# Three PSUM tiles cut by hand become one tile per buffer, and each weight block gets a DRAM tensor of its own

## The chip, the core and the metric

The kernel runs on one core of a Trainium2 chip. The metric is the device time of one execution in microseconds; the time before is the median of three runs.

## What is computed

An attention with a packed middle step feeds two matrix-multiply layers. Everything is float32 outside; inside, each operand of a large product is split into a rounded upper part and a small lower part, and three products (upper-upper, upper-lower, lower-upper) are added up in PSUM.

```python
# attention: 8 batches x 8 heads, 576 rows of 64, 32 packing rows
p_packed = sm_attn(p, k, v)               # softmax attention
out      = sm_attn(q, p_packed, p_packed)
x = out.transpose(0, 2, 1, 3).reshape(4608, 512)
# layer 1: 512 -> 2048 -> 512
h = x @ w_in
g = (a[0] + a[1]*h + a[2]*h**2 + a[3]*h**3) / (1 + abs(b[0])*abs(h) + abs(b[1])*h**2 + 1e-6)
x = g @ w_out
# layer 2: 512 -> 2048 -> 512
h = x @ w2_in
g = h * cos(h)
return g @ w2_out
```

## The kernel before, in words

The program is a list of steps (`add`), each with its engine, the objects that it reads, writes and makes, and the slots that its objects may take. `Plan.order` goes through an order of the steps per engine that is written out as numbers (`ORDER`), gives each new object a free slot (`make`), and emits the instructions in the order of the planned starts. Each engine runs its own list in order. The waits between engines are not written by hand: the framework derives them from the tiles that an instruction reads and writes.

PSUM has eight banks of 2 KB per partition. Before the change they are held by these tiles: `b2` (8192 bytes, four banks), `acc01` and `acc23` (two banks each, the latter in the place of the attention's `one0` and `one1`, which are tiles of their own, made anew for each use). `PART` says which slot is which slice of which tile, and `make` cuts the slice out by hand.

- Attention (the first 130 us, and parts of it later): `trans` (L946) transposes on TensorE into a slot of `tr`, that is `b2_0` or `b2_1`, the two halves of `b2`; `copied` (L950, ScalarE) reads it. `scores` (L973) writes the same slots; `max1`, `exp1`, `turn2` (L985, L991, L1050) read them. The transposes of exponents (L1008) and of small tiles (L960) write `one0` and `one1`.
- Layer 1 (128 items, up to about 1088 us): `front` (L1215) multiplies an attention half with folded weights into `b2_0` or `b2_1`, in turn; `absolute` (L1387) and `lin` (L1377) on ScalarE and `cubic` (L1382, L1384) on VectorE read the result. The rest of the rational function works in SBUF. `back` (L1235) adds the item into one of four accumulators `acc0` to `acc3`; at the end of a group `done1` (L1252 on ScalarE, L1250 on VectorE) empties them. `m_prod` (L1182) folds weights into a half of `b2`, emptied by L1191 and L1195.
- Layer 2 (six chunks of 768 tokens, eight quads each, from about 1088 us): in a quad, `part2` (L1270) makes seven products of six matmuls with 384 columns (a seven-product form of a two by two block product). Products 1, 6, 7 and 4 go one after another into one buffer A (slot `hA`, the first bank of `b2`), and after each of them `from_A` (L1280, ScalarE) copies A out; products 2, 5 and 3 go into a buffer B (slot `hB`, the second bank of `b2`), which `plus_B` (L1285, VectorE) adds to the copy. Then four cells of h times cos h run in SBUF (L1288 to L1316), and `back2` (L1324) adds each cell into three of six accumulators `six0` to `six5`. `six0` to `six3` lie in `acc01` and `acc23`, `six4` and `six5` in the third and fourth bank of `b2`. At the end of a chunk `done2` (L1335, L1337) empties all six.

The split weight blocks of layer 2 are written to DRAM during layer 1 (`b_keep`, L867) and read back for every quad (`b_back`, L870), seven blocks of 256 KB, into ten slots (`rg`) ahead of use. Before the change the seven blocks of a quad are slices of one DRAM tensor `w2[i]`, 128 rows of 14 KB, of which a block takes 2 KB.

Steps on engine "-" (`opening`) make slots available once the steps named have been issued, such as those of layer 2 in the place of layer 1's.

Of the kernel before, what the change touches and what calls it, by code (L numbers as in the profile page):

```python
# [10 lines left out]
F32 = mybir.dt.float32  # L11
# [565 lines left out]
def pack_attention_moe_moe_kernel(  # L577
# [14 lines left out]
    nc = tc.nc  # L592
# [1163 lines left out]
```

## Time and profile before

| what | us |
|---|---|
| median of three runs | 1967.95 |
| lowest, highest | 1960.86, 1969.67 |
| the profiled execution | 1970.45 |
| its span, from the first to the last instruction | 1968.7 |
| mean granted TensorE clock, share of full speed | 0.946 |

The profiled execution is the one that all rows come from; 1.75 us of its time lie outside the span. PE is TensorE's matmuls, PEld its weight loads, DVE VectorE, ACT ScalarE, POOL GpSimd, SP the engine that issues the DMAs. A group is written as line, engine, operation, output tile <- input tiles. Tiles appear by the program's names without numbers: `b` is the tile `b2`, `acc` is `acc01` or `acc23`, `one` is `one0` or `one1`, `ep` is the SBUF tile of the layers' work, `wo` and `g` the operands of `back` and `back2`. An idle time is put down to the instruction whose end released the engine. Matmul ends are modelled: a matmul's duration (0.3 to 0.4 us here) is longer than the distance to the next one, and after a wait the idle time shown is shorter than what the stream of matmuls lost.

### The profile page before, as it was taken

How to read it: one execution, taken by the hardware profiler on the slowest of the kernel's cores; microseconds unless marked ns; L12 is line 12 of the kernel's file. 1: busy time of each engine (PE TensorE's matmuls, PEld its weight loads, DVE VectorE, ACT ScalarE, POOL GpSimd, SP SyncE). 2: the span in 40 equal slices, each digit the busy share in tenths (PEclk: the TensorE clock that was granted, in tenths of full speed). 3: DMA queues.
4: the chain of work that ended last, by engine and by line, in shares of the span. 5: the costliest groups of instructions: out<-in, count | busy, mean ns of one | idle time of the engine just before them, and what ended most of it. 6: DMA issues, size and time to landing. Idle time of an engine off the chain costs nothing.

```text
span 1968.7 us, 28677 instructions
## 1 busy us (share of the span) xinstructions
PE 1665.3 (85%) x10416; PEld 1404.5 (71%) x10416; DVE 1376.1 (70%) x2434; ACT 1266.0 (64%) x2331; POOL 313.7 (16%) x287
## 2 busy tenths in 40 slices
PE   6666788887888888888898999988988888898988
PEld 3444577776877877777787777777777777776776
DVE  3445677878878878777887897667657657666665
ACT  4455667867777877777786776556556556556554
POOL 1222332212332322222220001001001000000000
PEclk8566899989999999999999999999999999999999
DMA  7545322323233112121125545335334434433431
GB/s 239 180 161 163 116 80 74 99 87 110 85 109 118 61 48 85 59 82 55 56 81 178 191 145 156 101 97 156 102 99 130 126 102 121 131 99 101 124 99 49
DMA packets 145165, 219.14 MB, mean 111 GB/s; under 512 B 25216, under 2 KB 77952, under 8 KB 145024
## 3 DMA queue, kind: packets, MB, share of 16 engines
q1 hardware_dynamic: 144448, 216.53, 36.3%
q8 instruction: 82, 1.34, 0.3%
q10 hardware_dynamic: 576, 0.79, 0.1%
q14 instruction: 59, 0.48, 0.1%
HBM read 173.21 MB, written 44.04 MB: 110 GB/s over the span
## 4 chain that ended last, share of the span: by engine, by line
PE 61%; ACT 18%; DVE 16%; issue 4%; DMA 1%; SPq 0%; DVEq 0%; ACTq 0%
PE b L1270 18%; PE acc L1324 12%; PE b L1215 11%; PE b L1324 7%; PE acc L1235 5%; DVE ep L1384 4%; ACT ep L1377 3%; DVE ep L1382 3%; ACT ep L1387 3%; PE b L946 3%; ACT ep L1280 3%; DVE ep L1285 2%; PE b L1182 2%; ACT ep L1390 2%; PE b L973 2%
## 5 line engine op out<-in xcount | busy, mean ns | idle before, releaser
L1235 PE MATMUL acc<-g,wo 128*128 128x288 f32 x3072 | 449.2, 300 | 23.2 <-ACT ob L1252 11.6
L1235 PEld LDWEIGHTS acc<-g,wo 128*128 128x128 f32 x3072 | 423.9, 191 | 52.4 <-ACT ob L1252 17.7
L1324 PE MATMUL acc<-wo,g 128*128 128x512 f32 x1152 | 306.3, 395 | 1.2 <-ACT st L1337 1.0
L1324 PEld LDWEIGHTS acc<-wo,g 128*128 128x128 f32 x1152 | 214.1, 188 | 32.8 <-ACT st L1337 1.4
L1280 ACT COPY ep<-b 128x384 f32<-128x384 f32 x192 | 91.9, 479 | 207.1 <-PE b L1324 117.0
L1296 DVE SCALAR_TENSOR_TENSOR ep<-ep 128x384 f32<-128x384 f32 x384 | 214.0, 559 | 6.7
L1396 POOL TENSOR_TENSOR ep<-ep 128x576 f32<-128x576 f32 x108 | 153.5, 1427 | 359.1 <-ACT ep L1390 130.0
L1324 PE MATMUL b<-wo,g 128*128 128x512 f32 x576 | 169.6, 408 | 42.4 <-ACT ep L1280 40.4
L1285 DVE TENSOR_TENSOR ep<-ep,b 128x384 f32<-128x384 f32 x144 | 79.6, 553 | 139.5 <-PE b L1324 89.9
L1324 PEld LDWEIGHTS b<-wo,g 128*128 128x128 f32 x576 | 101.1, 188 | 86.4 <-ACT ep L1280 72.6
L1288 ACT ACTIVATE ep<-ep 128x384 f32<-128x384 f32 x192 | 100.4, 524 | 85.8 <-DVE ep L1285 83.7
L1382 DVE TENSOR_TENSOR ep<-ep,b 128x576 f32<-128x576 f32 x128 | 93.9, 751 | 79.9 <-ACT ep L1387 40.4
L1310 DVE TENSOR_TENSOR ep<-ep 128x384 f32<-128x384 f32 x192 | 106.5, 557 | 58.1 <-ACT ep L1306 57.7
L1387 ACT ACTIVATE ep<-b 128x576 f32<-128x576 f32 x128 | 82.7, 648 | 96.9 <-PE b L1215 72.1
L1316 DVE TENSOR_TENSOR g<-ep,g 128x384 fp32r<-128x384 f32 x192 | 107.8, 563 | 42.1 <-ACT g L1313 41.9
L1215 PE MATMUL b<-a,sl2a 128*128 128x288 f32 x480 | 102.8, 326 | 38.5 <-DVE ep L1384 22.4
L1377 ACT ACTIVATE ep<-b,par 128x576 f32<-128x576 f32 x128 | 103.5, 828 | 44.6 <-PE b L1215 25.8
L1270 PE MATMUL b<-sr,a 128*128 128x384 f32 x518 | 115.9, 348 | 19.1 <-DVE ep L1285 11.0
L1384 DVE SCALAR_TENSOR_TENSOR ep<-ep,par,b 128x576 f32<-128x576 f32 x128 | 100.9, 810 | 43.9 <-PE b L1215 18.6
L1313 ACT CAST g<-ep 128x384 fp32r<-128x384 f32 x192 | 98.3, 513 | 48.8 <-DVE ep L1310 48.8
L1270 PE MATMUL b<-sr,sl2a 128*128 128x384 f32 x486 | 109.5, 350 | 19.3 <-DVE ep L1285 12.1
L1215 PE MATMUL b<-a,sr 128*128 128x288 f32 x576 | 95.6, 323 | 29.5 <-DVE ep L1384 12.2
(170 smaller groups left out, 3079.4 us busy)
## 6 DMA issues: line engine op xcount, KB each, us to landing
a<-w SPq DMA_DIRECT2D x135, 256.0 KB, 2.7
sl2a<-w SPq DMA_DIRECT2D x133, 256.0 KB, 2.7
sr<-w SPq DMA_DIRECT2D x68, 256.0 KB, 2.7
st<-in_moe_w_out_dram SPq DMA_DIRECT2D x32, 512.0 KB, 4.1
st<-in_moe_w_in_dram SPq DMA_DIRECT2D x30, 512.0 KB, 4.5
w<-fx SPq DMA_DIRECT2D x56, 256.0 KB, 2.0
x<-ob SPq DMA_DIRECT2D x24, 576.0 KB, 3.4
k_in<-in_k_dram SPq DMA_DIRECT2D x16, 576.0 KB, 5.4
```

What stands on the lines that cost most here:

```text
L1215: nc.tensor.matmul(TILE["h", j][:, e, 0:HS], lhsT=w[:, o : o + P], rhs=x[:, g, :], start=n == 0, stop=n == 3 * NG - 1,)
L1235: nc.tensor.matmul(o, lhsT=w, rhs=x, start=i == first and n == 0, stop=i == last and n == len(todo) - 1,)
L1270: nc.tensor.matmul(o, lhsT=u[:, ks], rhs=x[:, k, :], start=n in FRESH and k == 0 and j == 0, stop=k == KC // 2 - 1 and j == 2, skip_group_ ...
L1280: nc.scalar.copy(TILE["H", c, i, f, t], TILE["A", c, i][:, 0:W2])
L1285: nc.vector.tensor_tensor(H, H, B, op=ALU.add)
L1296: return nc.vector.scalar_tensor_tensor(Y, T, (-C1, -C2)[e], (TILE["H", *q], Y)[e], op0=ALU.mult, op1=ALU.add)
L1324: nc.tensor.matmul(o, lhsT=u[:, ms], rhs=x, start=FIRST2[c, t] == (i, f) and n == 0, stop=LAST2[c, t] == (i, f) and n == 2,)
L1377: nc.scalar.activation(shaped(j, "T"), hidden(j), AF.Identity, scale=par[:, 3:4], bias=par[:, 2:3])
L1382: nc.vector.tensor_tensor(T, T, h, op=ALU.mult)
L1384: nc.vector.scalar_tensor_tensor(T, T, par[:, 1:2], h, op0=ALU.add, op1=ALU.mult)
L1387: nc.scalar.activation(shaped(j, "V"), hidden(j), AF.Abs)
L1396: return side("denom", j).tensor_tensor(Q, Q, V, op=ALU.mult)
```

## The change

Each PSUM buffer becomes a tile of its own. Where a slot has no slab, `make` now asks the pool for a new tile under the slot's tag. `b2_0` and `b2_1` become tiles of two banks in the pool `ps2`, `acc0` to `acc3` tiles of one bank. For layer 2 the pool `ps2` is closed and a pool `ps4` opened in its place (`open_z`), with the tiles `hA`, `hB`, `six4` and `six5`; `six0` to `six3` use the tags of `acc0` to `acc3`. `open_z` runs once all steps `absolute`, `lin` and `cubic` have been issued, and `hA`, `hB`, `six4`, `six5` are free from then on; before, `hA` and `hB` came with the last `front`, and all of `six` with the first accumulator group that ended.

In DRAM `w2[i]` becomes seven tensors of 128 rows of 2 KB, one for each block.

The new opening step shifts the numbers of all later steps by one. Read with that shift, the order differs from before only in the passage from layer 1 to layer 2: 115 of 1760 TensorE steps change places, by at most 18 places, 188 of ScalarE's, 57 of SP's, and the like on VectorE; from the third quad of layer 2 on all orders are those of before. Five steps that may run on either engine change: three go from GpSimd to VectorE (a `denom`, an `x_less`, a `w_lo`) and two the other way (a `denom`, an `x_less`).

```diff
-    opened("ps2", space=PSUM)
+    yctx = ExitStack()
+    opened("ps2", yctx, space=PSUM, side="right")
     opened("aps", space=PSUM)
...
-        ("b2", "ps2", parts("b2", 4096, "b2_0", "b2_1")),
-        ("acc", "aps", parts("acc01", 2048, "acc0", "acc1")),
+        ("b2", "ps2", parts("ps2", 4096, "b2_0", "b2_1")),
+        ("acc", "aps", parts("aps", 2048, "acc0", "acc1")),
...
-        ("hA", "ps2", parts("b2", 2048, "hA")),
-        ("hB", "ps2", parts("b2", 2048, "hB", at=2048)),
-        ("six", "aps", parts("acc01", 2048, "six0", "six1") + parts("acc23", 2048, "six2", "six3") + parts("b2", 2048, "six4", "six5", at=4096)),
+        ("hA", "ps4", parts("ps2", 2048, "hA")),
+        ("hB", "ps4", parts("ps2", 2048, "hB", at=2048)),
+        ("six", "aps", parts("aps", 2048, *named("six", 4)) + parts("ps2", 2048, "six4", "six5", at=4096)),
...
-    SLOTS["acc"] += parts("acc23", 2048, "acc2", "acc3")
-    HOME |= dict.fromkeys(("acc2", "acc3"), "aps2")
+    SLOTS["acc"] += parts("aps", 2048, "acc2", "acc3", at=4096)
+    HOME |= dict.fromkeys(("acc2", "acc3", "six2", "six3"), "aps2") | dict.fromkeys(("six4", "six5"), "ps4")
+    TAG = {f"six{n}": f"acc{n}" for n in range(4)}
...
     def make(o, slot, shape, dt):
-        if slot not in PART:
-            TILE[o] = POOL[HOME[slot]].tile(shape, dt, tag=slot, name=slot)
+        key, at, _ = PART.get(slot, ("", 0, 0))
+        if key not in SLAB:
+            tag = TAG.get(slot, slot)
+            TILE[o] = POOL[HOME[slot]].tile(shape, dt, tag=tag, name=tag)
             return
-        key, at, _ = PART[slot]
...
-    w2 = dram("w2", NQ, [P, len(BLOCKS) * 2 * KW])
+    w2 = [{n: POOL["dp"].tile([P, 2 * KW], F32, name=f"w2_{i}_{n}") for n in BLOCKS} for i in range(NQ)]
...
-        nc.sync.dma_start(block_of(i, n), TILE["hl", i, n].bitcast(F32))
+        nc.sync.dma_start(w2[i][n], TILE["hl", i, n].bitcast(F32))
...
-        nc.sync.dma_start(TILE["rg", c, i, n].bitcast(F32), block_of(i, n))
+        nc.sync.dma_start(TILE["rg", c, i, n].bitcast(F32), w2[i][n])
...
-        slab("acc23", "aps2", 4096, F32)
...
+    def open_z():
+        yctx.close()
+        opened("ps4", space=PSUM, side="right", reuse_waits="tile")
...
-    opening(nothing, [s for s in steps_of("back") if s.args[0] == N1 - NPR], ("six",))
-    opening(open_y, [fronts[N1 - 1]], ("hA", "hB"), named("xg", 5))
+    opening(nothing, [s for s in steps_of("back") if s.args[0] == N1 - NPR], slots=named("six", 4))
+    opening(open_y, [fronts[N1 - 1]], slots=named("xg", 5))
+    opening(open_z, steps_of("absolute", "lin", "cubic"), ("hA", "hB"), ("six4", "six5"))
...
-    slab("b2", "ps2", 8192, F32)
-    slab("acc01", "aps", 4096, F32)
```

## Rows read from the trace of the kernel before

**Rows 1.** The page, part 1: engine, busy us, share of span, instructions.
```profile
PE 1665.3 (85%) x10416; PEld 1404.5 (71%) x10416; DVE 1376.1 (70%) x2434; ACT 1266.0 (64%) x2331; POOL 313.7 (16%) x287
```

**Rows 2.** Windows: length; busy PE, PEld, DVE, ACT, POOL; granted clock; DMA share; GB/s.
```profile
0.00:130.00 130.00, 84.66 (x872) 53.14 (x872) 52.98 (x111) 64.67 (x129) 25.80 (x38) 0.71 0.64 204
130.00:1088.00 958.00, 795.85 (x5935) 709.82 (x5935) 738.69 (x1127) 696.67 (x1154) 254.49 (x217) 0.93 0.29 93
...
1140.00:1925.00 785.00, 704.04 (x3239) 575.75 (x3240) 518.83 (x1065) 447.45 (x930) 33.37 (x33) 1.00 0.42 118
```

**Rows 3.** Chain of waits, share of the stretch by line: 130 to 1088, then 1140 to 1925.
```profile
by line: PE b L1215 22.4%; PE acc L1235 10.3%; DVE ep L1384 7.2%; ACT ep L1377 7.0%; DVE ep L1382 6.7%; ACT ep L1387 6.4%; issue 5.9%; PE b L1182 3.2%; ACT ep L1390 3.2%; DVE ep L1407 3.0%; PE b L946 2.5%; PE b L1270 2.0%; PE b L973 1.5%; A
...
by line: PE b L1270 40.0%; PE acc L1324 27.1%; PE b L1324 17.1%; ACT ep L1280 5.5%; DVE ep L1285 3.7%; issue 2.3%; ACT ep L1288 0.8%; ACT ep L1306 0.5%; DVE ep L1296 0.4%; DVE st L1335 0.4%; ACT ep L1302 0.3%; DVE ep L1310 0.3%; ACT g L1313
```

**Rows 4.** Chain of waits in order of time, in layer 2: start us, us, what.
```profile
1302.33 0.70 PE acc L1324 x3
...
1306.32 1.06 PE b L1270 x6
1307.38 0.71 PE b L1324 x3
...
1308.11 0.49 ACT ep L1280
```

**Rows 5.** Timeline in layer 2: start us, us, engine and group, [idle before <-releaser].
```profile
1506.33 0.86 PE L1324 MATMUL b<-wo,g 128*128 128x512 f32 x3
...
1507.23 0.48 ACT L1280 COPY ep<-b 128x384 f32<-128x384 f32 x1 [1.45 <-PE b L1324]
...
1507.76 0.97 PE L1324 MATMUL b<-wo,g 128*128 128x512 f32 x3 [0.57 <-ACT ep L1280]
```

**Rows 6.** Groups by line and shape, PE, 1140 to 1925: busy, mean, idle before.
```profile
L1324 PE MATMUL acc<-wo,g 128*128 128x512 f32 x1016 | 271.1, 395 | 0.2 <-DVE st L1335 0.2
L1324 PE MATMUL b<-wo,g 128*128 128x512 f32 x513 | 151.6, 409 | 39.0 <-ACT ep L1280 37.5 <-DVE ep L1285 1.4
```

**Rows 7.** Windows of line L1270 alone, 1140 to 1925: PE busy, PEld busy, clock.
```profile
1140.00:1925.00 785.00, 361.77 (x1710) 299.56 (x1710) 1.00 0.42 118
```

**Rows 8.** Waits of ACT and of DVE, 1140 to 1925: us in total, times, longest us.
```profile
ACT ep L1280 <- PE b L1324: 107.0, 74, 2.3
...
DVE ep L1285 <- PE b L1324: 81.3, 30, 2.9
```

**Rows 9.** Timeline in layer 1, two fronts on end and their readers.
```profile
425.78 2.84 PE L1215 MATMUL b<-a,sr 128*128 128x288 f32 x11
...
428.66 0.81 DVE L1384 SCALAR_TENSOR_TENSOR ep<-ep,par,b 128x576 f32<-128x576 f32 x1 [3.34 <-PE b L1215]
...
429.53 3.25 PE L1215 MATMUL b<-a,sr 128*128 128x288 f32 x12 [0.91 <-DVE ep L1384]
...
432.81 0.65 ACT L1387 ACTIVATE ep<-b 128x576 f32<-128x576 f32 x1 [6.12 <-PE b L1215]
```

**Rows 10.** Chain of waits in order of time, in layer 1.
```profile
708.57 1.80 PE b L1215 x12
...
717.25 1.60 PE acc L1235 x12
```

**Rows 11.** Waits of PE, 130 to 1088, first and seventh row.
```profile
PE b L1215 <- DVE ep L1384: 34.7, 30, 3.9
...
PE b L1182 <- ACT ep L1377: 5.6, 3, 2.3
```

**Rows 12.** Waits of PE, 0 to 130, first and seventh row.
```profile
PE b L946 <- ACT kT L950: 4.8, 5, 1.5
...
PE b L973 <- DVE sl2a L1195: 2.8, 1, 2.8
```

**Rows 13.** Groups by line and shape, PE, whole span: a tile of its own.
```profile
L1008 PE MATMUL one<-ident,e 128*128 128x128 f32 x64 | 15.4, 385 | 1.9 <-ACT e L991 1.8
```

**Rows 14.** The page, part 6: DMA issues, KB each, median us to landing.
```profile
a<-w SPq DMA_DIRECT2D x135, 256.0 KB, 2.7
```

More of the change, by code (lines that the diff above doesn't have):

```diff
@@ L860, in b_lo @@
         return side("b_lo", i, n).tensor_tensor(t[:, KW:], wsrc(i, n), t[:, 0:KW].bitcast(F32), op=ALU.subtract)
-    def block_of(i, n):
-        at = BLOCKS.index(n) * 2 * KW
-        return w2[i][:, at : at + 2 * KW]
     def b_keep(i, n):
-        nc.sync.dma_start(block_of(i, n), TILE["hl", i, n].bitcast(F32))
+        nc.sync.dma_start(w2[i][n], TILE["hl", i, n].bitcast(F32))
     def b_back(c, i, n):
-        nc.sync.dma_start(TILE["rg", c, i, n].bitcast(F32), block_of(i, n))
+        nc.sync.dma_start(TILE["rg", c, i, n].bitcast(F32), w2[i][n])
     SC = ([P, DM], U32)
```

410 rows, old and new, of tables (ON_DVE, ORDER) are left out of this document.

## The prediction, made before the changed kernel ran

> **What bounds the kernel now.** I read the page first: TensorE is busy for 85% of the span, VectorE for 70%, ScalarE for 64% [rows 1]. That looks like a kernel at its TensorE limit, but a matmul's shown duration overlaps the next one's, so I went on to the windows, cut where the work changes: attention alone up to 130 us, layer 1 up to 1088, layer 2 from there with its steady part 1140 to 1925 [rows 2]. Then, stretch by stretch, the chain of waits, which says what the end hangs on [rows 3], and last the waits and the timeline, to see which buffer each wait is about.
>
> In steady layer 2 the chain runs through TensorE for 84% (40.0, 27.1 and 17.1), and for 5.5% through L1280, 3.7% through L1285 and 2.3% through "issue", the hand-overs [rows 3]. L1280 and L1285 empty the product buffers A and B; they ought to hide behind other matmuls. What the stream of matmuls itself wants can be worked out: six of L1270 take 1.06 us in the chain, three of L1324 take 0.70 to 0.71 [rows 4], so 1710 of the one [rows 7] and 1016 + 513 of the other [rows 6] want 1710 x 0.177 + 1529 x 0.233 = 302 + 357 = 659 us of the 785. So 126 us of this stretch are not matmul stream.
>
> The timeline shows what eats them [rows 5]. Three matmuls of `back2` write tile `b` from 1506.33; `from_A` (L1280), which reads buffer A, also in tile `b`, starts only when they are done (released by PE b L1324 after 1.45 us idle); and the next three of `back2` on `b` wait for `from_A`. By the code `back2` writes `six4` and `six5`, the third and fourth bank of `b2`, and `from_A` reads the first: neither touches the other's data. The groups settle that it is the shared tile and not the cells: 1016 matmuls of the same line into `acc`, fed by the same cells, wait 0.2 us in all, 513 into `b` wait 39.0, of which 37.5 for L1280 [rows 6]. In the other direction ScalarE waits 107.0 us for L1324 on `b` before L1280, VectorE 81.3 before L1285 [rows 8]. So waits are kept for a whole tile, whatever slice of it is meant.
>
> Layer 1 has the same pattern. A front of 11 recorded matmuls on `b` runs from 425.78 to 428.62; its reader L1384 for the older item waits for it, the next front waits for L1384, and `absolute` (L1387), whose input was ready at 428.62, starts at 432.81, after the second front, with ScalarE idle for 6.12 us [rows 9]. Two L1387 follow each other, one per front, so the first had no reason to wait for the second front. In this stretch only 36% of the chain is L1215, L1235 and L1182, while the four readers of `b` (L1384, L1377, L1382, L1387) hold 27.3% and "issue" 5.9% [rows 3].
>
> A buffer that is a tile of its own behaves otherwise: `one0` and `one1` are such tiles, made anew for each use and alternating, and L1008 on them is idle 1.9 us in 64 matmuls, 1.8 of it for its input [rows 13].
>
> **The change part by part, against the profiled 1970.45 us.**
>
> *Layer 2.* `hA`, `hB`, `six4`, `six5` become tiles, so the waits of [rows 5, 6, 8] lose their cause. On the chain they are L1280, L1285 and issue, 11.5% of 785 = 90 us; the stretches 1088 to 1140 and 1925 to 1969 hold the same seven products and twelve cell parts per quad, 96 us in place of 785, so at the same share 11 us more: 101. What stays: a product into A must wait for the copy of the one before. That copy takes 0.49 us [rows 4], and the order puts product 2 or 5 (1.06 us) or cells between, which cover it; where nothing is between, 0.5 us shows. I take 95 us. Bounds: 60 if such real waits fill a third of the gap; 126 + 15 = 141 if the stream runs dense (the 126 us of [rows 4, 6, 7], scaled by 881/785). VectorE (519 of 785) and ScalarE (447) stay under a matmul stream of 659 plus what is left [rows 2].
>
> *Layer 1.* `b2_0`, `b2_1` and the four accumulators become tiles. Seven rows of waits of PE name a reader of `b` or `acc` as the releaser, 34.7 us the largest, 5.6 the last; they sum to 97.0 [rows 11]. Some are real: a front may only enter a half that the item two before has left. But the timeline shows that the readers themselves come late through the same waits [rows 9], so what is left of the real ones shrinks too, and each wait also costs the restart of the stream, which the idle time does not show. I take 110 us. Bounds: 40, if most waits turn out to be for the item two before; above, VectorE's 738.69 us [rows 2] are the floor, which leaves 958 - 739 = 219; I take 180 as the end, which would already have VectorE at 95% in place of 77%. The matmul stream is no floor before that: twelve of L1215 take 1.80 us and twelve of L1235 1.60 [rows 10], so 128 items of 12 + 24 want about 128 x 5.0 = 640 us, plus attention and folding.
>
> *Attention.* Six of the first seven rows of waits of PE up to 130 us are on `b`, for readers of the other half or of the same one, 24.2 us together, 4.8 the largest [rows 12]. The DMA share is 0.64 and no engine is busy for more than two thirds of it [rows 2], so this is a chain of latencies; I take 20 us, bounds 5 and 40.
>
> *Weight blocks in DRAM.* The same 256 KB move in the same pieces of 2 KB per partition, now from contiguous memory. A block lands 2.7 us after its issue [rows 14]; ten slots of products of 1.06 us [rows 4] lie ahead of use, and no DMA stands in the steady chain [rows 3]. Cost nil; if landing doubled to 5.4 it would still be covered, and if it halved nothing waits for it. The cover goes if landing exceeds about 10 us.
>
> *The passage to layer 2.* The new pool waits for the last readers of the last fronts where before it waited for the last front: two of four such readers take 0.65 and 0.81 us [rows 9], so 3 to 4 us, once, with `back` of the last items to fill it. The moved steps take or give at most the longest wait shown, 6 us. Three steps moved to VectorE against two moved off it are one more instruction of about 0.8 us. I take nil, bounds -6 and +10. No instruction is added or removed on a computing engine.
>
> Sum: 95 + 110 + 20 = 225, so 1970.45 - 225 = 1745.5 for the profiled execution; the median stood 2.5 lower, so 1743.
>
> **The rivals.**
>
> 1. *True waits take the place of the removed ones.* The gains go to their lower bounds: 60 + 40 + 5 = 105, time 1863; half-way between, with layer 2 as forecast and layer 1 at 40, 1820. For it: real dependences stand right behind (two halves of `b`, in-order engines, VectorE at 77% in layer 1 [rows 2]). Against it: the late reader's own input was four us old [rows 9]. I give the band 1800 to 1900 a chance of 0.17.
>
> 2. *More comes back than the waits.* In layer 1 the granted clock is 0.93, in steady layer 2 1.00 [rows 2], between the two levels 1.2 and 2.4 GHz; a front after idle time takes 3.25 us [rows 9] where one at full speed takes 1.80 [rows 10]. If layer 1 held 1.00, 7% of 958 = 67 us of full-speed time came back. With part of that and the dense bounds, 140 + 150 + 30 = 320, the time is 1650. Against it: VectorE's floor. 0.13 for less than 1690. The Trainium skill, TensorE: Matmul & The Clock Gate, Part 1: The HAM clock gate, says that the slow clock is the default and that activity releases it; by that rule fewer waits raise the clock, and the trace agrees as far as its busier stretch has the higher clock.
>
> 3. *The change does not do what it says.* If buffers of one pool were still ordered as one, or if the rotation over banks already overlapped all that can overlap, the time stays at 1968. Against it: the idle times of the groups [rows 6, 13]. 0.05. The Trainium skill, Perfetto Trace Analysis, Optimizing Tensor Performance: Matmuls, says that independent groups rotated through different banks let the emptying of one overlap the next group's matmuls; the kernel before does rotate, so by that rule nothing is left to gain here, and the timeline speaks against it: the banks differ and the work does not overlap [rows 5].
>
> 4. *Slower.* A tile made anew may enter its place only when the tile before it is released. If the release went by pool, each front would wait for the readers of the item just before, in place of the one two before. PE's waits for L1384 before L1215 are 34.7 us in 30 cases, 1.16 each [rows 11]; the other 98 fronts would pay it too, 113 us, and in layer 2 the waits stay: 2080. It decides from about nine fronts that wait anew without a gain elsewhere (10 us). Against it: L1008 on tiles of just this kind [rows 13]. 0.03.
>
> **How the numbers follow.** A difference of 0.5%, some 10 us, is about what a measurement of this kernel can tell from no change. The forecast band, 1690 to 1800, has 0.62. With rivals 1 and 2 at 0.17 and 0.13, faster has 0.92; same 0.05; slower 0.03. The range goes from 1655 to 1865: it takes in the forecast band, rival 1 down to its lower bounds and rival 2's 1650 nearly, and leaves out some 0.15.
>
> **What would show it.** Right: PE b L1324 waits no longer for L1280, and its idle time per matmul falls to that of the matmuls on `acc`; ScalarE no longer waits for L1324 before L1280; L1387 starts within a few tens of ns of its own front; L1280 and L1285 nearly vanish from the chain in layer 2; a quad of layer 2, 785 us over 1710/42 = 40.7 quads or 19.3 us now, nears 17. Layer 1 shorter by about 110 us with VectorE over 85% busy and a clock above 0.93. Wrong: the waits keep their sums under new names (rivals 1 and 4), or layer 1 stays at 958 us with VectorE as its end. What would make the forecast wrong is layer 1: its term has the widest bounds.

## The result and the profile after

The changed kernel takes 1571.78 us, the median of four runs from 1570.98 to 1574.60; the kernel before took 1967.39 beside it. The ratio is 0.7996, its 95% interval 0.7974 to 0.8018: 395.6 us less, where 225 were forecast. The profiled execution took 1570.98 us with a span of 1569.2; its mean granted clock is 0.997, where it was 0.946.

The page of after, part 1, answers [rows 1]:

```profile
PE 1517.6 (97%) x10416; PEld 1364.5 (87%) x10416; DVE 1372.4 (87%) x2435; ACT 1255.5 (80%) x2331; POOL 313.3 (20%) x286
```

TensorE is now busy for 97% of the span. VectorE's busy time is that of before (1372.4 to 1376.1 us) and ScalarE's 10 us less: the work is the same, only the time between its pieces is gone. In the windows of after (columns as in [rows 2]) attention ends at about 104, layer 1 at 838:

```profile
0.00:104.00 104.00, 79.86 (x1134) 53.02 (x1134) 73.45 (x152) 84.42 (x170) 36.96 (x50) 1.00 0.92 304
104.00:838.00 734.00, 712.66 (x5703) 661.99 (x5702) 717.72 (x1099) 672.52 (x1125) 242.68 (x203) 1.00 0.35 113
...
880.00:1535.00 655.00, 655.00 (x3243) 587.47 (x3242) 519.39 (x1061) 445.51 (x927) 33.63 (x33) 1.00 0.49 143
```

The granted clock is 1.00, the upper level of 2.4 GHz, in all three, where it was 0.71 and 0.93 in the first two. VectorE is busy for 717.7 of layer 1's 734 us, 98%. In layer 2 the matmuls fill every microsecond of 655.

To tell the stages apart in the same way in all kernels I use the starts of `back` and `back2`. In these answers for one line (columns: duration min/median/max in ns, first and last start in us) the two lines above the break are of before, on the trace that [rows 2] come from:

```profile
L1235 PE MATMUL acc<-g,wo x3072: 288/295/607, 166.2 to 1088.1; 128*128 128x288 f32 x192
L1324 PE MATMUL acc<-wo,g x1152: 387/397/632, 1091.7 to 1962.6; 128*128 128x512 f32 x192
```

The same two of after, whose numbers are one lower because a line above them went:

```profile
L1234 PE MATMUL acc<-g,wo x3072: 288/295/442, 100.3 to 824.1; 128*128 128x288 f32 x192
L1323 PE MATMUL acc<-wo,g x1152: 387/395/398, 830.9 to 1562.7; 128*128 128x512 f32 x192
```

| stage | before | after | difference |
|---|---|---|---|
| start to the first `back` | 166.2 | 100.3 | -66 |
| first to last `back` (layer 1) | 921.9 | 723.8 | -198 |
| last `back` to last `back2` (layer 2) | 874.5 | 738.6 | -136 |

These are the two profiled executions, which lie 399.5 us apart; the medians lie 395.6 apart.

The chain of waits of after, by line, for the stretches 104 to 838 and 880 to 1535, answers [rows 3]:

```profile
by line: PE acc L1234 33.0%; PE b L1214 17.9%; DVE ep L1406 4.3%; issue 4.1%; PE b L1181 2.7%; DVE ep L1381 2.6%; DMA st<-in_moe_w_in_dram 2.4%; DVE ep L1383 2.4%; DVE ep L1410 2.3%; ACT ep L1376 1.8%; DVE g L1416 1.8%; ACT ep L1386 1.5%; A
...
by line: PE acc L1323 35.8%; PE hA L1269 26.5%; PE hB L1269 19.7%; PE six L1323 18.0%
```

In layer 2 the chain is TensorE and nothing else; L1279 and L1284 (L1280 and L1285 of before), which held 9.2% of it, are gone from it. In layer 1 the four readers of `b` held 27.3% and now hold 8.3% (L1381 2.6, L1383 2.4, L1376 1.8, L1386 1.5). The groups by line and shape from 880 to 1535 answer [rows 6], and the waits of ScalarE there [rows 8]:

```profile
L1323 PE MATMUL acc<-wo,g 128*128 128x512 f32 x1012 | 268.3, 394 | 0.0
L1323 PE MATMUL six<-wo,g 128*128 128x512 f32 x510 | 132.2, 393 | 0.0
...
ACT ep L1279 <- PE hA L1269: 88.4, 130, 1.6
```

The cells that waited 39.0 us in `b` wait 0.0 in `six`, as those in `acc` always did. The copy of A still waits 88.4 us, but for `hA`, the product that it copies, in 130 cases; this is the true dependence, and the end doesn't hang on it: TensorE has no wait left in this stretch.

The timeline of layer 1 in after (start, duration, engine and group) answers [rows 9]. First TensorE, then ScalarE, in the same microseconds:

```profile
498.11 0.56 PE L1214 MATMUL b<-a,sl2a 128*128 128x288 f32 x3
...
500.91 0.56 PE L1214 MATMUL b<-a,sl2b 128*128 128x288 f32 x3
501.31 2.56 PE L1234 MATMUL acc<-g,wo 128*128 128x288 f32 x18
...
500.12 0.81 ACT L1376 ACTIVATE ep<-b,par 128x576 f32<-128x576 f32 x1
500.83 0.64 ACT L1386 ACTIVATE ep<-b 128x576 f32<-128x576 f32 x1
```

TensorE writes `b` without a gap from 498.11 to 501.47, while ScalarE reads `b` at 500.12 and 500.83 with no idle time before it. In the kernel before, the reader stood idle for 6.12 us until the other half had been written, too.

### The profile page after: what moved, and what is told of

Same layout as the page of the kernel before. It is cut to its first block, busy times and chain, and to the rows that moved or that the text cites. A ratio compares the mean times of both kernels' runs of the same rounds, so it can differ in the third digit from the quotient of the medians.

```text
span 1569.2 us, 28846 instructions
## 1 busy us (share of the span) xinstructions
PE 1517.6 (97%) x10416; PEld 1364.5 (87%) x10416; DVE 1372.4 (87%) x2435; ACT 1255.5 (80%) x2331; POOL 313.3 (20%) x286
## 4 chain that ended last, share of the span: by engine, by line
PE 74%; DVE 10%; ACT 7%; DMA 5%; issue 2%; SPq 1%; POOL 0%; ACTq 0%; DVEq 0%; POOLq 0%
PE acc L1323 17%; PE acc L1234 15%; PE hA L1269 13%; PE hB L1269 9%; PE six L1323 8%; PE b L1214 8%; DVE ep L1406 2%; DMA k_in<-in_k_dram 1%; DVE ep L1381 1%; PE b L1181 1%; DVE ep L1383 1%; DMA st<-in_moe_w_in_dram 1%; DVE ep L1410 1%; ACT ep L1376 1%; DVE g L1416 1%
## 5 line engine op out<-in xcount | busy, mean ns | idle before, releaser
L1234 PE MATMUL acc<-g,wo 128*128 128x288 f32 x3072 | 436.2, 297 | 4.1 <-DVE ob L1249 1.7
L1234 PEld LDWEIGHTS acc<-g,wo 128*128 128x128 f32 x3072 | 416.3, 188 | 25.5 <-issue 15.9
L1323 PE MATMUL acc<-wo,g 128*128 128x512 f32 x1152 | 304.8, 393 | 0.0
L1323 PEld LDWEIGHTS acc<-wo,g 128*128 128x128 f32 x1152 | 213.0, 188 | 30.4
L1279 ACT COPY ep<-hA 128x384 f32<-128x384 f32 x192 | 91.9, 479 | 97.0 <-PE hA L1269 96.7
L1323 PE MATMUL six<-wo,g 128*128 128x512 f32 x576 | 149.8, 393 | 0.0
L1301 ACT ACTIVATE ep<-ep 128x384 f32<-128x384 f32 x192 | 100.3, 523 | 41.2 <-DVE ep L1295 40.8
L1287 ACT ACTIVATE ep<-ep 128x384 f32<-128x384 f32 x192 | 100.5, 524 | 34.4 <-DVE ep L1284 32.9
L1323 PEld LDWEIGHTS six<-wo,g 128*128 128x128 f32 x576 | 107.1, 188 | 17.2
L1389 ACT ACTIVATE ep<-ep,par 128x576 f32<-128x576 f32 x128 | 110.9, 871 | 4.0 <-DVE ep L1410 2.5
L1376 ACT ACTIVATE ep<-b,par 128x576 f32<-128x576 f32 x128 | 104.2, 830 | 7.9 <-PE b L1214 4.6
L1284 DVE TENSOR_TENSOR ep<-ep,hB 128x384 f32<-128x384 f32 x144 | 79.3, 550 | 33.1 <-ACT ep L1279 29.7
L1305 ACT ACTIVATE ep<-ep 128x384 f32<-128x384 f32 x192 | 100.5, 525 | 5.1
L1406 DVE SCALAR_TENSOR_TENSOR ep<-ep,par 128x576 f32<-128x576 f32 x128 | 103.4, 813 | 0.2
L1383 DVE SCALAR_TENSOR_TENSOR ep<-ep,par,b 128x576 f32<-128x576 f32 x128 | 100.6, 807 | 2.8 <-ACT ep L1386 1.8
L1381 DVE TENSOR_TENSOR ep<-ep,b 128x576 f32<-128x576 f32 x128 | 93.0, 744 | 7.0 <-ACT ep L1386 6.1
L1406 DVE SCALAR_TENSOR_TENSOR ep<-ep 128x576 f32<-128x576 f32 x128 | 96.7, 760 | 0.2
```

What stands on the lines that cost most here:

```text
L1234: nc.tensor.matmul(o, lhsT=w, rhs=x, start=i == first and n == 0, stop=i == last and n == len(todo) - 1,)
L1323: nc.tensor.matmul(o, lhsT=u[:, ms], rhs=x, start=FIRST2[c, t] == (i, f) and n == 0, stop=LAST2[c, t] == (i, f) and n == 2,)
L1376: nc.scalar.activation(shaped(j, "T"), hidden(j), AF.Identity, scale=par[:, 3:4], bias=par[:, 2:3])
L1383: nc.vector.scalar_tensor_tensor(T, T, par[:, 1:2], h, op0=ALU.add, op1=ALU.mult)
L1389: nc.scalar.activation(shaped(j, "U"), shaped(j, "V"), AF.Identity, scale=par[:, 5:6], bias=par[:, 4:5])
L1406: return nc.vector.scalar_tensor_tensor(t, t, add_, shaped(j, "V"), op0=ALU.add, op1=ALU.mult)
```

## The experiments

Theory one, from the prediction: waits are kept for a whole tile, so slices of one tile in different banks wait for each other in both directions; the separate PSUM tiles are the whole gain. Its rivals: the new order of the passage, the three moved steps or the contiguous weight blocks bring part of it; or the clock brings it, and the waits are minor. Each edit is against the kernel after, unless it says otherwise. Line numbers are those of after.

**All slabs back.** Everything else of the change stays: order, engines, DRAM tensors.

```diff
-        yctx.close()
-        opened("ps4", space=PSUM, side="right", reuse_waits="tile")
+        pass
...
+    slab("acc01", "aps", 4096, F32)
+    slab("ps2", "ps2", 8192, F32)
```

(`acc23` comes back likewise, and `acc0` to `acc3` and `six0` to `six3` are its and `acc01`'s slices again.)

> The changed kernel with its PSUM buffers put back into three tiles; the new order of the steps in the passage and the weight blocks in DRAM tensors of their own stay. Theory (the waits kept per tile are all of the gain): the time of the kernel before, 1967 us, within 10. Rival (order, engine moves or the DRAM tensors carry a part): below 1950 us, and the gain that is missing is theirs.

Measured: 1966.93 us, ratio to before 0.9991 (0.9974 to 1.0009). All 395 us go back with the three slabs. With the three slabs in place, the order of the passage, the moved steps and the seven DRAM tensors are worth nothing that can be measured, so without tiles of their own for the buffers nothing of the gain is left. The other direction was not run: that these tiles alone, with the old order and one DRAM tensor per quad, bring the whole gain is not shown.

**One family at a time.** Layer 2's four tiles of `ps4` in one tile, halves and accumulators as after:

```diff
-        ("hA", "ps4", parts("ps2", 2048, "hA")),
-        ("hB", "ps4", parts("ps2", 2048, "hB", at=2048)),
+        ("hA", "ps4", parts("ps2 z", 2048, "hA")),
+        ("hB", "ps4", parts("ps2 z", 2048, "hB", at=2048)),
...
+        slab("ps2 z", "ps4", 8192, F32)
```

(`six4` and `six5` also become slices of `ps2 z`.)

> The changed kernel, but hA, hB, six4 and six5 are slices of one tile again, in layer 2 only. Theory: attention and layer 1 as in the changed kernel (last back of layer 1 at about 824 us), layer 2 back to its old length, 745 + 136 = 881 us, so 1572 + 136 = 1708 us, with PE waiting for L1279 before L1323 on the shared tile as before. Rival (layer 2 is shorter because layer 1 hands over earlier or the clock is higher): under 1640 us.

Measured: 1720.83 us, 149 more than after; ratio to before 0.8746 (0.8720 to 0.8771). The last `back` starts at 831.0, 7 us later than in after, and from there to the last `back2` at 1712.8 it is 882 us, 143 more than in after, so nearly all of the loss is in layer 2. The waits of TensorE and of ScalarE from 900 to 1500 are those of before again (total us, times, longest):

```profile
PE ps2 z L1323 <- ACT ep L1279: 27.8, 49, 0.6
PE ps2 z L1269 <- DVE ep L1284: 19.8, 24, 1.2
...
ACT ep L1279 <- PE ps2 z L1323: 83.1, 58, 2.3
```

Cells (L1323) wait for the copy of A, and the copy for cells, as in [rows 6, 8].

The two halves of `b2` in one tile, layer 2 and accumulators as after:

```diff
+    slab("ps2", "ps2", 8192, F32)
```

(`hA`, `hB`, `six4` and `six5` take another key in `PART`, so that they stay tiles.)

> The changed kernel, but the two halves b2_0 and b2_1 are slices of one tile again, in attention and layer 1 only. Theory: layer 2 as in the changed kernel (745 us), attention and layer 1 lose most of what they gained, 66 + 198 us, so 1572 + 220 to 264 = 1790 to 1836 us, granted clock in layer 1 near 0.93 again. Rival (the accumulators' tiles carry half of layer 1): 1700 us or less.

Measured: 1814.32 us, 242 more than after; ratio to before 0.9221 (0.9192 to 0.9249). The first `back` starts at 169.7 and the last at 1067.3, as in before within 4 and 21 us; from there to the last `back2` at 1808.2 it is 741 us, as in after. Attention and layer 1 thus owe nearly all to these two tiles. Its windows, and ScalarE's longest wait from 170 to 1068, are before's again:

```profile
0.00:170.00 170.00, 113.21 (x1101) 72.89 (x1102) 69.74 (x143) 82.95 (x164) 33.15 (x47) 0.74 0.58 187
170.00:1068.00 898.00, 755.96 (x5666) 684.53 (x5665) 712.42 (x1079) 669.16 (x1103) 245.46 (x207) 0.94 0.28 90
...
ACT ep L1386 <- PE ps L1214: 70.5, 32, 6.5
```

The clock falls back to 0.74 and 0.94 with the tile alone, so it follows the waits; how much of the loss goes through it is estimated further down. In layer 2 it can't be the cause: there it was 1.00 before and after.

The accumulators as slices of two tiles, the rest as after:

```diff
-        ("acc", "aps", parts("aps", 2048, "acc0", "acc1")),
+        ("acc", "aps", parts("acc01", 2048, "acc0", "acc1")),
...
+        slab("acc23", "aps2", 4096, F32)
...
+    slab("acc01", "aps", 4096, F32)
```

> The changed kernel, but acc0 to acc3 (and six0 to six3 in their place) are slices of two tiles again. The waits of PE for L1252 and L1250 before were 18.7 us. Theory: 10 to 40 us longer than the changed kernel, 1582 to 1612 us. Rival (accumulators carry half of layer 1's gain): 1670 us or more.

Measured: 1589.94 us, 18 more than after; ratio to before 0.8083 (0.8064 to 0.8102). In layer 1 `back` waits for `done1` (waits of PE, 102 to 838):

```profile
PE acc L1234 <- ACT ob L1251: 8.2, 15, 1.2
...
PE acc L1234 <- DVE ob L1249: 4.9, 8, 1.3
```

The three families give 149 + 242 + 18 = 409 us, against 395 for all together: they add up, with 14 us overlap.

**Which pair in layer 2?** First `hA` and `hB` in one tile, the cells' tiles apart; then `hA` with `six4` and `six5`, `hB` apart.

```diff
-        ("hA", "ps4", parts("ps2", 2048, "hA")),
-        ("hB", "ps4", parts("ps2", 2048, "hB", at=2048)),
+        ("hA", "ps4", parts("ps2 z", 2048, "hA")),
+        ("hB", "ps4", parts("ps2 z", 2048, "hB", at=2048)),
...
+        slab("ps2 z", "ps4", 4096, F32)
```

(In the second kernel `hA`, `six4` and `six5` take the key, `hB` doesn't, and the tile has 6144 bytes.)

> The changed kernel, but hA and hB are slices of one tile of two banks in layer 2; six4 and six5 stay tiles of their own. All four in one tile cost 149 us. In the trace of before PE's waits in the steady part split into 38.9 us before L1324 (against the accumulators) and some 36 before L1270 (between A and B, or both). Theory: roughly half of 149, 50 to 90 us, 1622 to 1662 us. Rival (the tie between products and cells is all): under 15 us.

> The changed kernel, but hA, six4 and six5 are slices of one tile in layer 2 and hB is a tile of its own. All four in one tile cost 149 us, hA with hB alone 42. Theory (the costs of the ties add up): the tie between A's copies and the cells' products is most of the rest, 60 to 107 us, 1632 to 1679 us, with PE waiting for L1279 before L1323 on the shared tile some 35 us. Rival (the ties only cost together): under 30 us.

Measured: 1613.99 us for the first (ratio 0.8200, 0.8173 to 0.8228), 42 more than after and under what was expected; 1645.36 for the second (0.8363, 0.8346 to 0.8380), 74 more. The waits of TensorE from 900 to 1500 in the second:

```profile
PE ps2 z L1323 <- ACT ep L1279: 30.8, 54, 0.6
```

So half of layer 2's loss is the copy of A against the cells, the pair of [rows 5] (this tile also ties `six4` to `six5`); 42 + 74 = 116 of 149. Counted from the last `back` to the last `back2` alone, the two take 773.5 and 810.1 us, 35 and 72 more than after, of 143. The 33 us left belong to B with the cells or to combinations, which wasn't tried apart.

**What sets layer 1 now?** VectorE's 98% or the matmul stream? `ratio` (L1410) on one column of each half lowers VectorE's busy time in layer 1 from 718 to 661 us; `back` without the product of the upper weights with the lower part of g takes 1024 of TensorE's matmuls; the third kernel does both, and the fourth relieves VectorE in the kernel before.

```diff
-        T = shaped(j, "T")
-        return nc.vector.scalar_tensor_tensor(T, shaped(j, "U"), 2.0, T, op0=ALU.subtract, op1=ALU.mult)
+        T, U = (shaped(j, n)[:, :, 0:1] for n in "TU")
+        return nc.vector.scalar_tensor_tensor(T, U, 2.0, T, op0=ALU.subtract, op1=ALU.mult)
```

```diff
-            todo += [(wh[:, ms], gh[:, e, :]), (wl[:, ms], gh[:, e, :]), (wh[:, ms], gl[:, e, :])]
+            todo += [(wh[:, ms], gh[:, e, :]), (wl[:, ms], gh[:, e, :])]
```

> The changed kernel with VectorE relieved in layer 1: the instruction of `ratio` (128 of them, about 0.68 us each) works on one column of 288 per half in place of all, which leaves that part of the function out; all waits and the order stay. About 80 us of VectorE's 718 in layer 1 go. Theory (VectorE sets layer 1 now, at 98% busy): 40 to 78 us shorter, 1494 to 1532 us. Rival (TensorE sets it, at 97%): less than 20 us shorter.

> The changed kernel with TensorE relieved in layer 1: `back` leaves out the product of the lower part of g (1024 of 3072 matmuls, 0.133 us each, 136 us of stream). Theory (VectorE sets layer 1): less than 20 us shorter. Rival (TensorE sets it): 60 us or more shorter. If both stand level, both this and the run with less VectorE work give under 30 us.

> The changed kernel with both reliefs of layer 1 at once: `ratio` on one column per half (some 57 us of VectorE's time in layer 1 went with it alone) and `back` without the product of the lower part of g (136 us of TensorE's stream). Alone they gave 4 us and minus 7 us. Theory (the two engines stand level in layer 1, and each hides the other's relief): 30 to 60 us shorter than the changed kernel, 1512 to 1542 us, with ScalarE, 92% busy there, as the next end. Rival (a third thing sets layer 1: the order, ScalarE, the loads): less than 15 us.

> The kernel before with the same relief of VectorE (`ratio` on one column per half). Theory (the waits per tile set layer 1 before, not VectorE): the 80 us of work give less than 30 us. Rival (VectorE was the floor before as well): 60 us or more.

| kernel | us | ratio to before | layer 1: us busy of VectorE and TensorE, clock (of 734 us from 104) |
|---|---|---|---|
| after | 1571.78 | 0.7996 (0.7974 to 0.8018) | 718, 713, 1.00 |
| VectorE relieved | 1568.00 | 0.7967 (0.7950 to 0.7984) | 661, 717, 1.00 |
| TensorE relieved | 1578.96 | 0.8022 (0.7998 to 0.8047) | 711, 605, 0.96 |
| both | 1555.24 | 0.7909 (0.7895 to 0.7922) | 640, 595, 0.97 (of 702) |
| before, VectorE relieved | 1961.37 | 0.9968 (0.9944 to 0.9993) | - |

The busy times are of a fixed window; from the first to the last `back` layer 1 takes 723.8 us in after, 714.6 with VectorE relieved, 728.5 with TensorE relieved and 702.0 with both. Relieving either engine alone moves nothing that the intervals of the whole time tell apart; relieving both gives 16 us, more than nothing and far under the 57 and more that were taken from each, between the bands of the two theories. The chain of waits by line, 300 to 800, shows the change of places: after, VectorE relieved, TensorE relieved:

```profile
by line: PE acc L1234 41.5%; PE b L1214 22.3%; DVE ep L1406 4.6%; issue 3.7%; DVE ep L1383 2.8%; DVE ep L1381 2.8%; PE b L1181 2.7%; DVE ep L1410 2.2%; DVE g L1416 1.7%; ACT ep L1376 1.3%; ACT ep L1389 1.2%; ACT ep L1386 1.2%; DMA st<-in_mo
```

```profile
by line: PE acc L1234 51.5%; PE b L1214 27.1%; PE b L1181 3.7%; issue 2.0%; DVE ep L1381 1.4%; DVE ep L1383 1.4%; ACT ep L1376 1.2%; DMA x<-ob 1.0%; DVE ep L1406 1.0%; ACT ep L1386 0.9%; DMA st<-a 0.9%; DMA ob<-x 0.8%; PE hA L1269 0.7%; DVE
```

```profile
by line: DVE ep L1406 18.1%; issue 11.4%; PE b L1214 8.8%; DVE ep L1381 8.6%; DVE ep L1383 8.4%; DVE ep L1410 8.1%; DVE g L1416 7.0%; PE acc L1234 5.2%; ACT ep L1376 2.0%; ACT ep L1386 1.9%; ACT ep L1389 1.7%; PE b L1181 1.6%; DVE sr L1194 
```

With VectorE relieved the chain is the matmul stream (51.5, 27.1 and 3.7%); with TensorE relieved it is VectorE (18.1% for L1406 and 7 to 9% for each of four more) and hand-overs. The windows 300 to 820 of after, and of the kernel with both reliefs, show the next in line:

```profile
300.00:820.00 520.00, 509.91 (x3897) 483.27 (x3897) 512.76 (x771) 474.55 (x779) 166.91 (x146) 1.00 0.32 103
```

```profile
300.00:820.00 520.00, 445.36 (x3183) 407.95 (x3184) 475.96 (x803) 482.11 (x810) 167.55 (x146) 0.97 0.34 108
```

ScalarE, busy for 475 of 520 us in after, is the busiest with 482. The chain with both reliefs has no line above 11.1% and runs through TensorE, ScalarE and VectorE alike. So layer 1 of after has two engines at 98% and a third at 91%, and no one of them is the end alone. How much of the 16 us ScalarE, and how much the lower clock of 0.97, holds back stays open. In before the relief gave about 6 to 9 us (by the interval, 1 to 11), under the 30 of its theory: VectorE, at 77%, was no floor there.

## Why the prediction was right in direction and wrong in size

*The mechanism.* The reading that the shared tile, and neither the cells nor the order, causes the waits was right: the slabs alone take the time back to 1967 us. The two edits costed at nil, DRAM blocks and passage, are nil beside the slabs; a block still lands 2.7 us after its issue. The signs listed for layer 2 came: L1323's idle time fell to 0.0 in both accumulators, the copies left the chain, and a quad takes 655 us over 1721 / 42 = 41.0 quads (1721 matmuls of L1269 in the window), 16.0 us, where "nears 17" was forecast.

*Layer 2: 95 forecast, 136 came* (143 to 149 by giving the slab back). The term that failed is the price read from the chain, 11.5% or 101 us. It counted L1280, L1285 and "issue" alone. TensorE held 84.2% of the chain, 661 us of 785, about the 659 that the stream wants; all the rest, 15.8% or 124 us, was time that the stream stood still. The cells (L1288 to L1313) and the emptying of `six` (L1335) are part of it, since they follow a late copy on the same engines. That is the gap of 126 us found by the other way, and all of it went: in after the chain of this stretch is TensorE alone. "What stays", 6 us of the 101, was a small mistake in the same direction: with `hA` free, the products and cells between cover every copy, and L1269 and L1323 have no wait in 655 us. The upper bound, "141 if the stream runs dense", was the answer: 659 us were worked out for the steady stretch, and after needs 655 for nearly the same matmuls (3243 to 3239).

*Attention and layer 1: 20 + 110 forecast, 66 + 198 came* (242 by the halves, 18 by the accumulators). The table of stages cuts at the first `back`, the prediction at 130 us. The matmul that follows the 872 before 130 us starts at 130.1 in the kernel before and at 81.8 in after; ScalarE and VectorE pass the same place at 82.2 and 83.0. So in the prediction's own borders attention gave 48 us and layer 1 216. The term that failed is the sum of TensorE's idle rows, 97.0 and 24.2. It counts one engine (and of that the first rows only). ScalarE waited for fronts as well; the waits of ScalarE before (130 to 1088) and after (104 to 838; total us, times, longest):

```profile
ACT ep L1387 <- PE b L1215: 72.1, 33, 6.6
ACT ep L1377 <- PE b L1215: 25.8, 20, 3.6
...
ACT ep L1386 <- PE b L1214: 7.3, 10, 1.5
ACT ep L1376 <- PE b L1214: 4.6, 9, 1.4
```

What is gone of them, 86 us, went with the shared tile, so it was for fronts whose data the reader didn't need; TensorE's next front in turn waited for those late readers. That is a loop through three engines, of which the rows of one engine show only its own part. The chain of [rows 3] erred to the other side: four readers and "issue" held 33.2% of 958, 318 us, because it also holds work of the readers that is still done. The prediction named a better measure and cut it: VectorE's 738.69 us as floor, the least that its own work needs, gave 219, and the end was set at 180 because that "would already have VectorE at 95%". VectorE runs at 98%, and in these borders layer 1 takes 742 us, 216 less.

*The range* ended at 1655 us and 1571.78 came. The upper bounds of the three terms, 141 + 180 + 40 = 361, would have reached 1607; rival 2, which set the end, took 150 and 30 of the last two. With 219 uncut the bounds make 400 and 1568. So the range failed by the cut of layer 1's bound and by not adding the bounds up; attention's 40 was too low as well.

*Attention* was sized at 20 by the same idle rows. Here the loads are the likely floor; no run took bytes away. In the windows up to and from the first `back` of the kernel before,

```profile
0.00:166.00 166.00, 110.76 (x1097) 71.41 (x1098) 69.27 (x142) 82.58 (x164) 33.77 (x46) 0.68 0.60 190
166.00:1088.00 922.00, 769.75 (x5711) 691.55 (x5711) 722.40 (x1096) 678.76 (x1120) 246.52 (x208) 0.95 0.29 92
```

the DMA share of 0.60 is 100 us of transfers, and the first `back` of after starts at 100.3, with a DMA share of 0.92 up to 104. In the chain of after from 0 to 104 the loads of k, p and q hold 33.7%:

```profile
by line: DMA k_in<-in_k_dram 21.2%; DMA p_in<-in_p_dram 8.5%; PE b L945 5.4%; ACT kT L949 4.5%; DMA q_in<-in_q_dram 4.0%; issue 3.9%; DVE r L1049 3.7%; ACT qT L949 3.7%; PE b L972 3.6%; PE one L1022 2.5%; ACT e1T L1014 2.4%; DVE st L817 2.4
```

Floors taken stage by stage from before, 0.60 x 166 = 100 for attention, VectorE's 722 for layer 1, and 659 / 785 x 874.5 = 734 for the stream of layer 2, add up to 1556; with the 6 us from the last `back2` to the end of the span and the 2 outside it 1564, 8 under the time measured. That sum is made in hindsight, and only from rows of before.

*Rival 1* (true waits take the place) fell: the seven largest rows of TensorE's waits in layer 1 had 97.0 us, and the largest of after is 4.2 (waits of PE, 104 to 838: total us, times, longest):

```profile
PE b L1214 <- DVE ep L1383: 4.2, 6, 2.0
PE b L1181 <- DVE sr L1194: 3.5, 2, 3.2
```

*Rival 2* (more comes back) came nearest, and the gain went past its 320 too. The clock rose from 0.93 to 1.00 in layer 1 as it said. How much of the 198 us is the clock's own: among the starts of L1215 and L1235, 376 of 4548 neighbouring matmuls of before stood 225 to 255 ns apart, where most stand 133 apart, and 73 of 4549 in after. Each is 106 ns longer, so 303 x 0.106 = 32 us. Not all of them are the clock's: some 240 of the 376, and 13 of the 73, stand where the granted clock was at the lower level of 1.2 GHz, which gives 24 us. So 24 to 32 us is an estimate from the starts; no run held the waits and changed the clock. Its objection, "VectorE's floor", was sound, only the floor of 739 us lay below the 778 that the cut end left.

*Rival 3* (no gain) fell. The Trainium skill, Perfetto Trace Analysis, Optimizing Tensor Performance: Matmuls, asks for independent groups rotated over different banks, so that emptying one overlaps the next. With all slabs back the kernel still rotates so, and takes 1966.93 us; the same banks as tiles of their own take 1571.78. The measurement decides: different banks weren't enough here, as long as they were slices of one tile. *Rival 4* (release by pool) fell as well: it asked for 98 more fronts that wait 1.16 us each, and fronts wait for L1383 in six cases, 4.2 us in all.

## What to carry to other kernels

Where waits are derived from tiles, give each PSUM buffer that is filled and emptied on its own a tile of its own: in this kernel a slice in another bank of the same tile was ordered against its neighbours, in both directions. To size the gain of removed false waits, don't add up one engine's idle rows, and don't price a chain by the releasers alone; take, stage by stage, the busy time of the busiest resource (TensorE's as the distance between matmuls, not their shown durations) as the floor and ask which true dependence keeps the stage above it. Don't cut that floor because a share near 100% seems too much. Here the sum of floors came within 8 us, but worked out afterwards and for this one kernel.

## What the runs showed of the hardware that was not expected

- VectorE can stay busy for 717.7 of 734 us beside a TensorE that is busy for 712.7; matmuls followed each other for 655 us without a wait that the profile shows.
- Taking a third of `back`'s matmuls away made layer 1 no shorter: TensorE's busy time fell from 712.7 to 605.1 us, and the granted clock of the stretch from 1.00 to 0.96. The Trainium skill, TensorE: Matmul & The Clock Gate, Part 1: The HAM clock gate, has the clock follow how busy TensorE has been; the row agrees. The time by rows: 1578.96 with fewer matmuls, 1571.78 with all.
